# A second load queue, another split of the row means and a longer fill in the prologue of a fused attention and GLU kernel

## The chip, the cores and the metric

The kernel runs on one core of a Trainium2 chip. The metric is the time of one execution on the device in microseconds (us); a smaller number is better. The kernel before took 219.8 us in the median of three runs (219.64 to 220.88). Engines are named as the profile names them: TensorE (PE, with its weight loader PEld), VectorE (DVE), ScalarE (ACT), GpSimd (POOL) and SyncE (SP), which here issues DMA transfers.

## The reference

For 2048 tokens of width 512, in bfloat16, the reference adds three things: the input `x`, a linear attention branch and a bilinear gated branch. Both branches read the layer norm of `x`.

```python
xn = _layernorm(x)                                   # (x - mean) / sqrt(var + 1e-5)
q, k, v = split(xn @ wqkv)                           # 32 heads of 16
phi(a) = concat(softmax(a @ w_phi), softmax(-(a @ w_phi)))
kv = sum over tokens of phi(k) x v;  z = sum of phi(k)
attn = (phi(q) @ kv) / (phi(q) @ z + 1e-6) @ wo
glu  = ((xn @ w_gate) * (xn @ w_up)) @ w_down        # inner width 1792
out  = x + attn + glu
```

## The kernel before

The tokens are 16 tiles of 128 rows. All data stand in one on-chip array, `arena`, and all matrix products in eight banks of `ps`. The kernel is recorded as a list of steps, each with its engine, what it reads and writes, an estimated cost and latency; a DMA has an estimated landing time, its `at`. `_order` (L793) plays the list through with these estimates and fixes the order of the steps on every engine; a step that is marked `urgent` goes first when it could start within 300 ns (50 ns on TensorE) of the candidate. `_emit_all` (L847) then writes the instructions in that order with semaphore waits. So an estimate has no effect on the chip but through the order. In the profile nearly all matmuls have line L297, copies by ScalarE L277 and DMA issues L165 or, with a transpose, L164, as helpers record them.

The prologue is the stretch up to the first gate and up products:

- Loads (L352 to L364), all issued by SP: tile 0 of `x`, tile 1, tiles 2 and 3 together, the value weights in two halves (`wv`), the first four column blocks of the gate and up weights (`load_gu`), the feature map weights, tiles 4 to 7, and the key projection weights by a transposing DMA (`load_wT`).
- VectorE clears a block called `zero`, and TensorE multiplies it with itself 27 times into a bank that is not read (L367 to L369); four more such matmuls follow tile 1 (L734). This document calls them fills.
- For each of tiles 0 to 3 (`RAW = 4`) `emit_centred` (L418) subtracts the row mean. VectorE takes mean and variance with two instructions (L415, L416) and subtracts (L430). For tile 1 (`ACT_MEAN`) ScalarE instead takes the mean by a copy that sums its row (L423), VectorE subtracts, and the variance is taken later.
- `emit_T` (L474) transposes the centred tile by four matmuls with the identity (the prediction calls them T0 to T3), and ScalarE copies the bank to `xnT`. Later tiles are transposed by DMA.
- `k_pe` (L552) projects the tile on the value weights in four matmuls (K0 to K3 in the prediction), each of which reads a quarter of `xnT` of that tile and a quarter of `wv`; the first two need the first half of `wv`, the others the second. GpSimd raises the variance to the power of -1/2 meanwhile (L437, L439), and that scales the projection when it is copied out.
- `wprime` (L493) folds the feature map into the key projection weights.

After the prologue TensorE alternates key features, value projections and the GLU's gate and up products, later query features, and ends with the output products (`final`, L684) of all tiles.

The lines that record the fills, and those of tile 1's mean:

```python
    dve(lambda e: e.memset(zero, 0.0), [], [zero], 128)
    mms([(bank(7, 0, 128), zero, zero, True, True)] * 27, cold=True)
...
            sc.step(ACT, lambda e: e.activation(out=xn_tile(t), in_=x_tile(t), func=ACTF.Copy, scale=1.0 / 512.0,
                                                accum_out=mean),
```

Of the kernel before, what the change touches and what calls it, by code (L numbers as in the profile page):

```python
# [5 lines left out]
BF16 = mybir.dt.bfloat16  # L6
F32 = mybir.dt.float32
ACTF = mybir.ActivationFunctionType
# [4 lines left out]
PE, ACT, DVE, POOL, SP = "PE", "ACT", "DVE", "POOL", "SP"  # L13
# [6 lines left out]
NT = S_TOK // 128  # L20
NQ = D // 128
# [160 lines left out]
def bass_parallel_sum__linear_kernel_hedgehog__glu_gated_bilinear__prompt_kernel(  # L182
    nc: bass.Bass,
    A_x: bass.AP,
    A_wqkv: bass.AP,
    A_w_phi: bass.AP,
    A_wo: bass.AP,
    B_x: bass.AP,
    B_w_gate: bass.AP,
    B_w_up: bass.AP,  # L190
    B_w_down: bass.AP,
    out: bass.AP,
):
    with ExitStack() as es:
        _build(nc, es, A_x, A_wqkv, A_w_phi, A_wo, B_w_gate, B_w_up, B_w_down, out)


def _build(nc, es, A_x, A_wqkv, A_w_phi, A_wo, B_w_gate, B_w_up, B_w_down, out):
# [59 lines left out]
    def sbv(name, lo, n):  # L258
        off = layout[name] + lo
        return arena[:, off:off + n]  # L260

    def sbf(name, lo_f32, n_f32):
        off = layout[name]
        return arena[:, off:off + 2 * (lo_f32 + n_f32)].bitcast(F32)[:, lo_f32:lo_f32 + n_f32]

    def bank(b, lo=0, n=512):
        return psum[:, b * 512 + lo: b * 512 + lo + n]

    sc = _Sched(nc)


    def act_op(out_ap, in_ap, func=ACTF.Copy, scale=1.0, bias=None, prio=None):
        def fn(e):
            kw = {}
            if bias is not None:
                kw["bias"] = bias
            return e.activation(out=out_ap, in_=in_ap, func=func, scale=scale, **kw)  # L277
        r = [in_ap]
        if isinstance(scale, bass.AP):
            r.append(scale)  # L280
        if isinstance(bias, bass.AP):
            r.append(bias)
        return sc.step(ACT, fn, reads=r, writes=[out_ap], cost=(50.0 if str(in_ap.tensor.name) == "ps" else 95.0) + 0.833 * in_ap.free_size(),
                       lat=180.0, prio=prio)

    def dve(fn, reads, writes, n, rate=1.0, fixed=65.0, prio=None):
        return sc.step(DVE, fn, reads=reads, writes=writes, cost=fixed + rate * n / 0.96, lat=150.0, prio=prio)
# [4 lines left out]
    def mms(items, prio=None, cold=False):  # L292

        def fn(e):
            ins = None
            for o, l, r, a, z in items:
                ins = e.matmul(o, lhsT=l, rhs=r, start=a, stop=z)  # L297
            return ins
        reads = []
        writes = []  # L300
        c = 0.0
        for o, l, r, a, z in items:
            reads += [l, r]
            writes.append(o)
            c += max(25.0, o.free_size() / 2.4 + 2.3) * (1.92 if cold else 1.0)
        return sc.step(PE, fn, reads=reads, writes=writes, cost=c, lat=260.0, prio=prio)
# [12 lines left out]
    def x_tile(t):  # L319
        return sbv("x", t * 512, 512)  # L320

    xnT_v = sbv("xnT", 0, NQ * S_TOK).rearrange("p (q s) -> p q s", q=NQ)
# [5 lines left out]
    wv_v = sbv("wv", 0, NQ * 512).rearrange("p (q j) -> p q j", q=NQ)  # L328
# [7 lines left out]
    def load_x(on, t0, n, at):  # L336
        return sc.dma(on, sbv("x", t0 * 512, n * 512).rearrange("p (t d) -> p t d", t=n),
                      x_flat[t0 * 128:(t0 + n) * 128, :].rearrange("(t p) d -> p t d", p=128), at=at)

    def load_w(on, dst, src, at, issue=500.0):  # L340
        return sc.dma(on, dst, src, at=at, issue=issue)
# [5 lines left out]
    def load_gu(on, f0, n, at):  # L347
        return [load_w(on, v[:, :, f0 * 128:(f0 + n) * 128],
                       src[:, f0 * 128:(f0 + n) * 128].rearrange("(q p) f -> p q f", p=128), at)
                for v, src in ((wg_v, B_w_gate), (wu_v, B_w_up))]  # L350

    load_x(SP, 0, 1, 2950.0)  # L352
    load_x(SP, 1, 1, 3400.0)
    load_x(SP, 2, 2, 4700.0)
    wv_loads = [load_w(on, wv_v[:, 2 * h:2 * h + 2, :],
                       A_wqkv[h * 256:(h + 1) * 256, 1024:1536].rearrange("(q p) j -> p q j", p=128), at)
                for on, h, at in ((SP, 0, 5700.0), (SP, 1, 6600.0))]
    load_gu(SP, 0, 4, 9300.0)
    sc.dma(SP, wphi_v, bass.AP(tensor=A_w_phi.tensor, offset=A_w_phi.offset, ap=[[16, 128], [2048, NQ], [1, 16]]),
           at=10900.0)  # L360
# [3 lines left out]
    load_gu(SP, 9, 5, 22300.0)  # L364


    zero = sbv("tree", 0, 128)  # L367
    dve(lambda e: e.memset(zero, 0.0), [], [zero], 128)  # L368
    mms([(bank(7, 0, 128), zero, zero, True, True)] * 27, cold=True)  # L369


    def c_fn(e):
# [30 lines left out]
    mv_v = sbf("mv", 0, NT * 2).rearrange("p (t k) -> p t k", t=NT)  # L403
# [10 lines left out]
    def emit_moments(t):  # L414
        dve(lambda e: e.bn_stats(stats_v[:, t, 0:6], x_tile(t)), [x_tile(t)], [stats_v[:, t, 0:6]], 512)  # L415
        dve(lambda e: e.bn_aggr(mv_v[:, t, :], stats_v[:, t, 0:6]), [stats_v[:, t, 0:6]], [mv_v[:, t, :]], 6)  # L416

    def emit_centred(t):  # L418

        reads = [x_tile(t)]  # L420
        if t in ACT_MEAN:
            mean = lnt_v[:, 2, 8 + t:9 + t]
            sc.step(ACT, lambda e: e.activation(out=xn_tile(t), in_=x_tile(t), func=ACTF.Copy, scale=1.0 / 512.0,  # L423
                                                accum_out=mean),
                    reads=[x_tile(t)], writes=[xn_tile(t), mean], cost=720.0, lat=180.0)
            reads.append(xn_tile(t))
        else:
            mean = mv_v[:, t, 0:1]
            emit_moments(t)
        dve(lambda e: e.tensor_scalar(out=xn_tile(t), in0=x_tile(t), scalar1=mean, scalar2=None,  # L430
                                      op0=ALU.subtract), reads + [mean], [xn_tile(t)], 512, rate=0.5)

# [3 lines left out]
    def emit_root(t):  # L436
        pool(lambda e: e.tensor_scalar(out=veps(t), in0=mv_v[:, t, 1:2], scalar1=1e-5, scalar2=None, op0=ALU.add),  # L437
             [mv_v[:, t, :]], [veps(t)], 1)
        pool(lambda e: e.tensor_tensor(out=rstd_v[:, t, 0:1], in0=veps(t), in1=mhalf[:, 0:1], op=ALU.pow),  # L439
             [veps(t), mhalf], [rstd_v[:, t, 0:1]], 1, rate=155.0, fixed=400.0)  # L440
# [22 lines left out]
    def xn_tile(t):  # L463
        return sbv("xn", (t % 4) * 512, 512)
# [4 lines left out]
    def next_a():  # L469
        b = a_bank[0] % a_banks[0]  # L470
        a_bank[0] += 1
        return b

    def emit_T(t):  # L474
        b = (5, 6, 7, 4)[t] if t < RAW else next_a()
        mms([(bank(b, q * 128, 128), xn_tile(t)[:, q * 128:(q + 1) * 128], ident, True, True) for q in range(NQ)],
            cold=t < 2)
        act_op(xnT_v[:, :, t * 128:(t + 1) * 128], bank(b).rearrange("p (q s) -> p q s", q=NQ))

    def emit_xn(t):  # L480
        dve(lambda e: e.tensor_scalar(out=xn_tile(t), in0=x_tile(t), scalar1=mv_v[:, t, 0:1],  # L481
                                      scalar2=rstd_v[:, t, 0:1], op0=ALU.subtract, op1=ALU.mult),
            [x_tile(t), mv_v[:, t, 0:1], rstd_v[:, t, 0:1]], [xn_tile(t)], 512, rate=0.5)
        if t >= 4:
            sc.dma(SP, xnT_v[:, :, t * 128:(t + 1) * 128], xn_tile(t), transpose=True, issue=1250.0, land=3200.0,
                   at=36000.0 + 1300.0 * (t - 8) if t >= 8 else 23600.0 + 550.0 * (t - 4))
            return
        emit_T(t)
# [63 lines left out]
    def k_pe(t):  # L552
        b = next_a()
        items = group(bank(b), [(xnT(q, t * 128, 128), wv_v[:, q, :]) for q in range(NQ)])
        if t < RAW:
            for item in items:
                mms([item])
        else:
            mms(items)
        act_op(vext_all[:, t, :, 0:64], bank(b).rearrange("p (c j) -> p c j", c=8), scale=scale_of(t))  # L560
# [166 lines left out]
    for t in range(RAW):  # L727
        first = len(sc.steps)
        emit_centred(t)
        emit_T(t)  # L730
        for st in sc.steps[first:]:
            st.urgent = True
        if t == 1:
            mms([(bank(7, 0, 128), zero, zero, True, True)] * 4, cold=True).deps.append(sc.by_eng[PE][-2])  # L734
        if t in ACT_MEAN:
            emit_moments(t)
        emit_root(t)
        k_pe(t)
# [192 lines left out]
```

## Time and profile before

| what | us |
|---|---|
| median of three runs | 219.8 (219.64 to 220.88) |
| the profiled execution | 219.75 |
| its span, first instruction to last | 218.5 |
| TensorE busy, share of the span | 213.9, 98% |
| VectorE busy | 193.0, 88% |
| ScalarE busy | 115.8, 53% |
| GpSimd busy | 10.7, 5% |
| DMA moved | 19.91 MB, 91 GB/s in the mean |

The busy time of an engine is an average over stages with different limits; the profile's row of 40 slices (5.46 us each) and its chain of waits tell which engine limits a stage. A line of the chain, and one of the timeline, starts with its start and its length in us. In the timeline "x4" is the number of instructions that are merged, and what stands in brackets is the idle time of the engine before them and what ended it. The time of an overlapped group is from its first start to its last end, so a matmul's own latency is in it once.

### The profile page before, as it was taken

Reading aid. Unit: us, or ns where it says so; the run is one execution under the profiler, and the core shown is the slowest. Engines: PE = TensorE matmul, PEld = TensorE weight load, DVE = VectorE, ACT = ScalarE, POOL = GpSimd, SP = SyncE. Lnnn points to the kernel's source line nnn. Section 1 sums busy time; section 2 is a strip of 40 time slices with the busy share of each in tenths; the row PEclk is TensorE's granted clock in tenths of the full one; section 3 lists DMA queues with packets and bytes.
Section 4 is the critical chain, followed back from the end, with each engine's and each line's share of the span. In section 5 each row is a group of like instructions: output and inputs, shape, how many; then the busy total and the mean of one; then the engine's idle time right before and its main releaser. Section 6 shows DMA issues by size and latency. Waiting matters only on the chain.

```text
span 218.5 us, 3596 instructions
## 1 busy us (share of the span) xinstructions
PE 213.9 (98%) x1290; PEld 105.0 (48%) x1313; DVE 193.0 (88%) x549; ACT 115.8 (53%) x191; POOL 10.7 (5%) x29
## 2 busy tenths in 40 slices
PE   7999999999999999999999999999999999999996
PEld 7444444444445544444445544444544444454454
DVE  4577999999999389999998899999999999999532
ACT  4658987538443599965553687553444353121000
POOL 4532000010002000000000000000000000000000
DMA  6999540025900440000000002273456548546931
GB/s 172 316 238 354 100 172 4 0 52 147 329 3 13 85 99 0 0 0 3 0 0 1 3 0 48 48 99 74 96 116 128 106 110 106 123 111 126 139 76 48
DMA packets 47458, 19.91 MB, mean 91 GB/s; under 512 B 37456, under 2 KB 47440, under 8 KB 47440
## 3 DMA queue, kind: packets, MB, share of 16 engines
q1 hardware_dynamic: 47440, 19.69, 40.4%
q8 instruction: 10, 0.16, 0.3%
q14 instruction: 8, 0.07, 0.1%
HBM read 8.67 MB, written 2.10 MB: 49 GB/s over the span
## 4 chain that ended last, share of the span: by engine, by line
PE 95%; DMA 2%; issue 1%; SPq 1%; ACT 1%; DVE 0%
PE ps L297 95%; DMA arena<-in_A_wqkv_dram 2%; SPq L165 1%; ACT arena L277 1%; DVE arena L703 0%
## 5 line engine op out<-in xcount | busy, mean ns | idle before, releaser
L297 PE MATMUL ps<-arena 128*128 128x512 bf16 (+4 forms) x1290 | 213.9, 327 | 2.8 <-DVE arena L368 1.0
L297 PEld LDWEIGHTS ps<-arena 128*128 128x128 bf16 (+1 forms) x1313 | 105.0, 99 | 111.5 <-issue 1.1
L277 ACT ACTIVATE arena<-ps 128x512 bf16<-128x512 f32 (+1 forms) x136 | 71.8, 583 | 47.1 <-PE ps L297 40.2
L277 ACT ACTIVATE arena<-arena 128x1024 bf16<-128x1024 bf16 (+1 forms) x40 | 38.5, 977 | 30.1 <-DVE arena L528 29.9
L542 DVE TENSOR_TENSOR arena<-arena 128x512 f32<-128x512 bf16 (+3 forms) x128 | 48.8, 392 | 0.2
L598 DVE TENSOR_TENSOR arena<-ps,arena 128x512 bf16<-128x512 f32 x56 | 38.3, 683 | 5.8 <-PE ps L297 4.7
L522 DVE TENSOR_TENSOR arena<-arena 128x64 bf16<-128x64 bf16 (+3 forms) x128 | 31.5, 271 | 3.8 <-ACT arena L277 3.5
L528 DVE TENSOR_TENSOR arena<-arena 128x1024 bf16<-128x1024 bf16 x32 | 21.7, 680 | 0.1
L703 DVE TENSOR_TENSOR arena<-ps,arena 128x512 bf16<-128x512 f32 (+2 forms) x13 | 8.3, 642 | 7.1 <-PE ps L297 7.1
L574 DVE TENSOR_TENSOR arena<-arena 128x1024 bf16<-128x1024 bf16 x16 | 10.8, 678 | 0.0
L277 ACT ACTIVATE arena<-ps,arena 128x512 bf16<-128x512 f32 x12 | 7.8, 681 | 2.6 <-PE ps L297 2.6
L571 DVE RECIPROCAL arena<-arena 128x64 bf16<-128x64 f32 x16 | 8.7, 544 | 0.0
L675 DVE TENSOR_TENSOR arena<-ps,arena 128x512 bf16<-128x512 f32 x12 | 8.1, 678 | 0.1
L452 DVE BATCH_NORM_STATS2 arena<-arena 128x6 f32<-128x512 bf16 x12 | 8.0, 684 | 0.0
L667 DVE RECIPROCAL arena<-ps 128x32 f32<-128x32 f32 x16 | 5.6, 349 | 1.8 <-PE ps L297 1.8
L654 DVE TENSOR_TENSOR arena<-arena 128x512 bf16<-128x512 bf16 x16 | 6.6, 415 | 0.0
L651 DVE RECIPROCAL arena<-arena 128x32 f32<-128x32 f32 x16 | 5.4, 338 | 0.0
L481 DVE TENSOR_SCALAR arena<-arena 128x512 bf16<-128x512 bf16 x12 | 4.3, 400 | 0.7 <-POOL arena L460 0.7
L415 DVE BATCH_NORM_STATS2 arena<-arena 128x6 f32<-128x512 bf16 x4 | 2.8, 690 | 2.1 <-DMA arena<-in_A_x_dram 2.0
L458 POOL TENSOR_SCALAR arena<-arena 128x4 f32<-128x4 f32 x3 | 0.8, 257 | 52.2 <-DVE arena L454 52.2
L460 POOL TENSOR_TENSOR arena<-arena 128x4 f32<-128x4 f32 x3 | 3.1, 1049 | 0.2
L700 DVE SCALAR_TENSOR_TENSOR arena<-ps,arena 128x512 bf16<-128x512 f32 x4 | 3.0, 748 | 0.1
(29 smaller groups left out, 24.4 us busy)
## 6 DMA issues: line engine op xcount, KB each, us to landing
out_dram<-arena SPq DMA_DIRECT2D x15, 128.0 KB, 1.9
arena<-in_B_w_down_dram SPq DMA_DIRECT2D x1, 1792.0 KB, 7.5
arena<-in_B_w_gate_dram SPq DMA_DIRECT2D x2, 640.0 KB, 6.6
arena<-in_B_w_up_dram SPq DMA_DIRECT2D x2, 640.0 KB, 7.8
arena<-in_A_x_dram SPq DMA_DIRECT2D x1, 1024.0 KB, 5.7
arena<-arena SPq DMA_TRANSPOSE x44, 2.6
arena<-in_A_wqkv_dram SPq DMA_DIRECT2D x2, 256.0 KB, 3.9
arena<-in_B_w_gate_dram SPq DMA_DIRECT2D x1, 512.0 KB, 5.7
```

The costliest lines, as they stand in the source:

```text
L277: return e.activation(out=out_ap, in_=in_ap, func=func, scale=scale, **kw)
L297: ins = e.matmul(o, lhsT=l, rhs=r, start=a, stop=z)
L452: dve(lambda e, t=t: e.bn_stats(stats_v[:, t, 0:6], x_tile(t)), [x_tile(t)], [stats_v[:, t, 0:6]], 512)
L522: dve(lambda e, dst=dst, src=src, k=k: e.tensor_tensor(out=dst, in0=src[:, :, 0:k], in1=src[:, :, k:2 * k], op=ALU.max), [src], [dst], 16 ...
L528: dve(lambda e: e.tensor_tensor(out=p4, in0=p4, in1=src[:, :, None, :].to_broadcast([128, 16, 16, 4]), op=ALU.subtract), [pst, src], [pst] ...
L542: dve(lambda e, dst=dst, src=src, k=k: e.tensor_tensor(out=dst, in0=src[:, :, 0:k], in1=src[:, :, k:2 * k], op=ALU.add), [src[:, :, 0:2 * ...
L571: dve(lambda e: e.reciprocal(out=rs, in_=sm), [sm], [rs], 64, rate=6.0)
L574: dve(lambda e: e.tensor_tensor(out=e4, in0=e4, in1=r4[:, :, None, :].to_broadcast([128, 16, 16, 4]), op=ALU.mult), [ek_v[:, t, :], rs], [ ...
L598: dve(lambda e: e.tensor_tensor(out=dst, in0=bank(bu), in1=gr, op=ALU.mult), [bank(bu), gr], [dst], 512, prio=-1.0)
L654: dve(lambda e: e.tensor_tensor(out=e1, in0=e1, in1=rs[:, :, None, :].to_broadcast([128, 8, 16, 4]), op=ALU.mult), [e1, rs], [e1], 512, ra ...
L675: dve(lambda e: e.tensor_tensor(out=o4, in0=n4, in1=w4, op=ALU.mult), [nd[:, :, 0:64], w], [o], 512)
L703: dve(lambda e: e.tensor_tensor(out=og, in0=ob, in1=xs, op=ALU.add), [ob, xs], [og], c1 - c0, prio=-2.0)
```

## The change

- Tile 2 and tile 3 of `x` are loaded apart. Tile 3 and the second half of the value weights are issued by ScalarE, behind a one-element copy that the change puts first on ScalarE (`first`); both DMAs wait for this copy. The estimated landing times of these loads change with it.
- The fills read a constant of ones that is there from the program's start, and VectorE's clear goes. There are 32 instead of 27 at the start, and two behind T0 and two behind T1 instead of four behind T1.
- For tile 1 ScalarE takes the negative mean and subtracts it in a second activation; VectorE's subtraction of that tile goes.
- The copy of a transposed tile to `xnT` is made in two halves of 256 columns each.

```diff
--- before.py
+++ after.py
@@ -349,12 +349,18 @@
                        src[:, f0 * 128:(f0 + n) * 128].rearrange("(q p) f -> p q f", p=128), at)
                 for v, src in ((wg_v, B_w_gate), (wu_v, B_w_up))]
 
+    def load_v(on, h, at):
+        return load_w(on, wv_v[:, 2 * h:2 * h + 2, :],
+                      A_wqkv[h * 256:(h + 1) * 256, 1024:1536].rearrange("(q p) j -> p q j", p=128), at)
+
     load_x(SP, 0, 1, 2950.0)
     load_x(SP, 1, 1, 3400.0)
-    load_x(SP, 2, 2, 4700.0)
-    wv_loads = [load_w(on, wv_v[:, 2 * h:2 * h + 2, :],
-                       A_wqkv[h * 256:(h + 1) * 256, 1024:1536].rearrange("(q p) j -> p q j", p=128), at)
-                for on, h, at in ((SP, 0, 5700.0), (SP, 1, 6600.0))]
+    load_x(SP, 2, 1, 4000.0)
+    first = sc.step(ACT, lambda e: e.activation(out=sbf("lnt", 2 * NT + 15, 1), in_=nc.const_aps.tensor(1.0, [128, 1], BF16),
+                                                func=ACTF.Copy), writes=[sbf("lnt", 2 * NT + 15, 1)], cost=1350.0)
+    load_x(ACT, 3, 1, 4400.0).deps.append(first)
+    load_v(SP, 0, 5300.0)
+    load_v(ACT, 1, 5800.0).deps.append(first)
     load_gu(SP, 0, 4, 9300.0)
     sc.dma(SP, wphi_v, bass.AP(tensor=A_w_phi.tensor, offset=A_w_phi.offset, ap=[[16, 128], [2048, NQ], [1, 16]]),
            at=10900.0)
@@ -364,9 +370,8 @@
     load_gu(SP, 9, 5, 22300.0)
 
 
-    zero = sbv("tree", 0, 128)
-    dve(lambda e: e.memset(zero, 0.0), [], [zero], 128)
-    mms([(bank(7, 0, 128), zero, zero, True, True)] * 27, cold=True)
+    one = nc.const_aps.tensor(1.0, [128, 128], BF16)
+    mms([(bank(7, 0, 128), one, one, True, True)] * 32, cold=True)
 
 
     def c_fn(e):
@@ -420,13 +425,14 @@
         reads = [x_tile(t)]
         if t in ACT_MEAN:
             mean = lnt_v[:, 2, 8 + t:9 + t]
-            sc.step(ACT, lambda e: e.activation(out=xn_tile(t), in_=x_tile(t), func=ACTF.Copy, scale=1.0 / 512.0,
+            sc.step(ACT, lambda e: e.activation(out=xn_tile(t), in_=x_tile(t), func=ACTF.Copy, scale=-1.0 / 512.0,
                                                 accum_out=mean),
                     reads=[x_tile(t)], writes=[xn_tile(t), mean], cost=720.0, lat=180.0)
-            reads.append(xn_tile(t))
-        else:
-            mean = mv_v[:, t, 0:1]
-            emit_moments(t)
+            sc.step(ACT, lambda e: e.activation(out=xn_tile(t), in_=x_tile(t), func=ACTF.Identity, bias=mean),
+                    reads=[x_tile(t), xn_tile(t), mean], writes=[xn_tile(t)], cost=522.0, lat=180.0)
+            return
+        mean = mv_v[:, t, 0:1]
+        emit_moments(t)
         dve(lambda e: e.tensor_scalar(out=xn_tile(t), in0=x_tile(t), scalar1=mean, scalar2=None,
                                       op0=ALU.subtract), reads + [mean], [xn_tile(t)], 512, rate=0.5)
 
@@ -475,7 +481,8 @@
         b = (5, 6, 7, 4)[t] if t < RAW else next_a()
         mms([(bank(b, q * 128, 128), xn_tile(t)[:, q * 128:(q + 1) * 128], ident, True, True) for q in range(NQ)],
             cold=t < 2)
-        act_op(xnT_v[:, :, t * 128:(t + 1) * 128], bank(b).rearrange("p (q s) -> p q s", q=NQ))
+        for q in range(0, NQ, 2):
+            act_op(xnT_v[:, q:q + 2, t * 128:(t + 1) * 128], bank(b, q * 128, 256).rearrange("p (q s) -> p q s", q=2))
 
     def emit_xn(t):
         dve(lambda e: e.tensor_scalar(out=xn_tile(t), in0=x_tile(t), scalar1=mv_v[:, t, 0:1],
@@ -730,8 +737,8 @@
         emit_T(t)
         for st in sc.steps[first:]:
             st.urgent = True
-        if t == 1:
-            mms([(bank(7, 0, 128), zero, zero, True, True)] * 4, cold=True).deps.append(sc.by_eng[PE][-2])
+        if t < 2:
+            mms([(bank(7, 0, 128), one, one, True, True)] * 2, cold=True).deps.append(sc.by_eng[PE][-2])
         if t in ACT_MEAN:
             emit_moments(t)
         emit_root(t)
```

## The prediction

> **What bounds the kernel now.** I read the chain that ended last first, then the page's busy row of TensorE, then the timeline of the first 16 us, engine by engine, because the diff touches nothing that runs later.
>
> The chain over the whole span, as the page shares it out, and the page's busy row:
>
> ```profile
> PE   7999999999999999999999999999999999999996
> ...
> PE 95%; DMA 2%; issue 1%; SPq 1%; ACT 1%; DVE 0%
> ```
>
> TensorE is full in every slice but the first and the last, and 95% of the chain is its matmuls. Nothing in the diff changes how many matmuls run after the prologue, so the change is worth what it takes from, or adds to, the time at which TensorE starts its unbroken run. The chain cut to the first 25 us shows where that lies:
>
> ```profile
> 2.69 4.46 DMA arena<-in_A_wqkv_dram
> ...
> 7.20 0.82 PE ps L297 x3
> ...
> 8.08 6.66 PE ps L297 x33
> 14.76 0.61 ACT arena L277
> ...
> 15.45 9.66 PE ps L297 x44
> ```
>
> The last wait of the prologue is the second half of the value weights (wv1): issued at 2.69, landed 4.46 later. From 7.20 TensorE runs without a real hole; the stop at 14.76 is the copy of the folded weights, which the change leaves as it is. The timeline gives the feeders:
>
> ```profile
> 0.78 1.28 ACT L423 ACT_TABLE_LOAD   x1 [0.78 <-PEq L916]
> 1.03 3.06 PE L297 MATMUL ps<-arena 128*128 128x128 bf16 x27 [1.03 <-DVE arena L368]
> 2.18 0.98 SPq L165 DMA_DIRECT2D arena<-in_A_wqkv_dram  x2
> 3.39 0.63 ACT L423 ACTIVATE arena<-arena 128x512 bf16<-128x512 bf16 x1 [1.33 <-DMA arena<-in_A_x_dram]
> 3.89 0.68 DVE L430 TENSOR_SCALAR arena<-arena 128x512 bf16<-128x512 bf16 x2
> 3.92 0.19 ACT L423 ACTIVATION_READ_ACCUMULATOR arena<-arena 128x1 f32 x1
> 4.69 0.69 DVE L415 BATCH_NORM_STATS2 arena<-arena 128x6 f32<-128x512 bf16 x1
> 5.64 0.35 DVE L430 TENSOR_SCALAR arena<-arena 128x512 bf16<-128x512 bf16 x1
> 7.20 7.03 PEld L297 LDWEIGHTS ps<-arena 128*128 128x128 bf16 x37 [0.45 <-DMA arena<-in_A_wqkv_dram]
> 10.03 4.20 PEld L297 LDWEIGHTS ps<-arena 128*128 128x128 bf16 x20
> 14.65 0.90 PEld L297 LDWEIGHTS ps<-arena 64*128 64x128 bf16 x35 [0.42 <-issue]
> ```
>
> And three narrow cuts of TensorE give its two speeds:
>
> ```profile
> 5.34 0.42 PE L297 MATMUL ps<-arena 128*128 128x128 bf16 x2
> 5.70 0.94 PE L297 MATMUL ps<-arena 128*128 128x512 bf16 x2
> 8.08 0.39 PE L297 MATMUL ps<-arena 128*128 128x128 bf16 x4
> ```
>
> Two early 128-column matmuls span 0.42, and the 27 fills give (3.06-0.31)/26 = 0.106 apart; four late ones in 0.39 are 0.056 apart. The 512-column pair at 5.70 is 0.38 apart, three at 7.20 in 0.82 are 0.216 apart. So the array doubles its pace at about 6.45; the granted clock reads 1.00 throughout and does not show it. The weight loader's 0.45 before 7.20 is its wait for wv1. In order: T0, T1 (transposes of x 0 and x 1) from 4.30 to 5.13, four fills, value projection K0 from 5.70, T2, a hole from 6.92 to 7.20, T3 at 8.08, then nine K matmuls, 8.30+9x0.216 = 10.24, where the first gate matmul starts (its weights load from 10.03). The 20 gate and up matmuls then reach 14.56. Every microsecond by which 10.24 moves, the end moves, as long as the up weights (issued at 3.72, 6.9 to landing: 10.6) and the transposed key weights are there.
>
> **The change, part by part.** Order first, from the planner's own rules worked by hand (for order alone): fills, T0, two fills, T1, two fills, T2, K0 (4), one of K1, T3, the rest of K1, K2, K3, gate. T2 goes ahead of K0 because it is marked urgent and due within the planner's 0.05. The gate's planned start hardly moves, so the order behind it should stay.
>
> *Fills on ones.* The clear on VectorE (0.87 to 0.98) goes; TensorE need not wait until 1.03 but can start at about 0.80, since the other engines' first instructions start at 0.78. 32 fills at 0.107 end at 4.22, before T0 can start at 4.30; started at 1.03 they would end at 4.45 and cost 0.15. I take nothing, nearest to the 0.78 rows. The hole 3.89 to 4.30 closes. Whether a closed hole doubles the pace earlier no row shows: between nothing and all cold work after 4.30. I take nothing, the pace doubling at 6.45 again.
>
> The Trainium skill, in "TensorE: Matmul & The Clock Gate" (Part 1), says that the clock gate opens after a busy window of about 3.4 us, that the window runs free and that the point moves by 0.5 us from run to run. By it the closed hole is no promise: this trace doubled about 5.4 after its first matmul, hole and all.
>
> *x 2 apart.* x 2 and x 3 came in one 256 KB load, issued at 1.71 and 3.0 to landing (4.7), and stats of x 2 waited for it until 4.69. 128 KB alone, by x 1's spacing (0.44 behind x 0), lands at about 3.8. VectorE also loses x 1's subtraction, so stats 2 starts when x 0's is through, 4.22: stats 0.69, aggregate 0.18, subtract 0.35 with gaps as now give 5.52 instead of 5.99, and x 3 6.79 instead of 7.20. x 3 comes from ScalarE's issue at about 2.4 plus 2.1 to 3.0 (the x rows), 4.5 to 5.4: beside stats 2 until about 5.49, and it costs if later.
>
> *Second half of wv and x 3 on ScalarE.* Table load to 2.06, the small copy 0.23 (the 128x65 copy's row), x 3's issue 0.42, wv1's 0.47, with gaps: ScalarE is free at about 3.3, x 1 lands at 3.37, so the mean starts at 3.39 as now. Behind these two issues on ScalarE stand x 1's mean and subtraction, for which T1 and everything behind it wait: that is the cover, 0.07 thick. SP passes one issue less, so gate and up weights, key-projection weights, x 4 to 7 and the long transpose issue 0.5 earlier; bytes bind there (290 GB/s from 3.5 to 6.5, 333 to 10.5), so I give them nothing. wv1's issue moves from 2.69 to about 2.85, but it no longer queues behind wv0: x 2, x 3 and both halves are 768 KB, at 290 to 333 GB/s from 3.4 all in by 5.8 to 6.1. K0's third matmul is due at 6.64, so the hole at 6.92 goes. If wv1 is as late as now (7.16), 0.5 of it returns.
>
> *Mean 1 and subtraction on ScalarE.* The accumulator is read by 4.11; a second 512-wide activation is 0.63 (SBUF row) and 0.09 for its per-partition operand (0.688 against 0.597 on L277): 4.15 to 4.87. The subtraction leaves VectorE (0.35). T1 may start at 4.92 instead of 4.70; the first two fills fill 4.71 to 4.92.
>
> *Copies in halves.* A copy of 512 columns is 0.60, its successor 0.49 later; a half is between 0.30 and 0.40. The first half of x 0's copy is ready at about 5.35 instead of 5.55, but K0 now waits for T2, so no gain; the extra 0.07 per tile on ScalarE lies beside TensorE.
>
> *Sum.* T1 4.93 to 5.35, fills to 5.57, T2 (ready 5.57) slow to 6.00, K0's first at 6.00, second at 6.42, third (fast) at 6.64, fourth 6.86, K1's first 7.07, T3 7.29 to 7.51, eleven K matmuls 2.37: 9.88. Against 10.24 that is 0.36 earlier. The up weights are needed at 10.75 and landed at 10.6; the folding at 14.30 needs the transposed weights, on hand before 14.65 and issued 0.5 earlier. Span 218.5 becomes 218.15; the profiled execution took 219.75, 1.25 more than its span and 0.05 under the median, so I forecast 219.4.
>
> **Rivals.** *ScalarE is late (slower, 0.18).* The trace shows ScalarE idle from 2.06 to 3.39; it shows no instruction that could have started in between. If the engine accepts nothing until up to 3.39, then copy and two issues run to 4.55, the mean to 5.30, the subtraction to 6.06, T1 at 6.11 with TensorE empty from 4.92. From there 0.43 (T1), 0.11, 0.22, K and T3 3.67: 10.54, 0.30 late, and wv1, issued at 4.1 and 3.4 to 4.5 to landing (the two wv rows), comes 7.5 to 8.6 where 7.30 is wanted. Together 0.3 to 1.3 late, near 220.4. It decides from the point at which ScalarE is free 0.36 later than 3.39. Against it: x 1 landed at 3.37, which explains the wait by itself.
>
> The Trainium skill, "ScalarE: Activation LUTs" (What ACT_TABLE_LOAD costs), speaks for this one: it puts a drain of about 1.38 us behind the load's 1.283. The load agrees to the digit; the drain would end at 3.44, where the trace starts an ACTIVATE at 3.39, so at most 1.33 fits, and no row can show less.
>
> *Issue slower on ScalarE, or wv1 late: no gain (0.19).* The issues on L165 took 0.40 to 0.89; at 0.6 to 0.65 each ScalarE is free at 3.7 and the 0.36 is gone. wv1 at 7.16 leaves 0.1 to 0.2 at best. 219.6 to 219.9.
>
> *The pace doubles early (0.12).* If the closed hole brings it by 5, T2 ends at 5.8, all K at 0.216: 9.45. The gate runs to 10.31, the up weights hold it to 10.3 to 10.6: 0.5 to 0.8 gained, 218.9 to 219.2.
>
> *Not what it says, or another order behind (0.03).*
>
> **Chances.** Forecast 219.1 to 219.6: 0.48. A measurement tells about 1% from no change, 2.2 us: 217.6 and 222.0. The prologue holds no 2.2 to win (its holes and slow matmuls after 4.30 are under 1.5), and the slow rival ends at 221.0; so 0.02 faster, 0.93 within, 0.05 slower for what I have not seen. Range 218.9 to 220.7: from the early pace to most of the late ScalarE.
>
> **What would show it.** Right: first gate weights load near 9.7 instead of 10.03, no hole before K0's third matmul, mean 1 on ScalarE at 3.4, stats 2 at 4.2. Wrong: ScalarE's first DMA issue later than 2.6, T1 after 5.0, wv1 landing after 6.6, or a hole anywhere behind 15 us.

## The result

The changed kernel took 222.48 us in the median of eight runs (220.99 to 225.26), the kernel before 219.88 (219.47 to 220.88): 1.0096 times as long, with a 95% interval of 1.0074 to 1.0118. (One run, 225.26, is left out of the ratio as disturbed.) The forecast was 219.4, with a range that ended at 220.7. The profiled execution took 222.71 with a span of 221.5, which is 3.0 more than the span before.

The page's row of TensorE and its clock row, of the kernel after:

```profile
PE   8699999999999999999999999999999999999996
...
PEclk9799999999999999999999999999999999999999
```

The holes are still in the first two slices alone, but there is a clock row now: the page before had none. The chain cut to the first 22 us (start, length, what):

```profile
0.78 1.28 ACT L359
...
2.08 0.21 ACT arena L359
...
2.31 0.39 ACTq L165
...
2.73 5.58 DMA arena<-in_A_wqkv_dram
8.31 0.14 issue
8.45 13.56 PE ps L297 x87
```

It runs through the moved load from end to end: table load, small copy, issue of x 3, and then the second half of the value weights (wv1), issued at 2.73, as before (2.69), and landed 5.58 later instead of 4.46. The timeline has the rest:

```profile
3.67 0.63 ACT L428 ACTIVATE arena<-arena 128x512 bf16<-128x512 bf16 x1 [1.39 <-DMA arena<-in_A_x_dram]
4.22 0.69 DVE L420 BATCH_NORM_STATS2 arena<-arena 128x6 f32<-128x512 bf16 x1
5.21 0.40 PE L297 MATMUL ps<-arena 128*128 128x128 bf16 x4 [0.20 <-ACT arena L431]
6.16 0.69 DVE L420 BATCH_NORM_STATS2 arena<-arena 128x6 f32<-128x512 bf16 x1 [0.65 <-DMA arena<-in_A_x_dram]
6.45 0.59 PE L297 MATMUL ps<-arena 128*128 128x512 bf16 x2 [0.48 <-DMA arena<-in_A_wqkv_dram]
8.45 13.78 PE L297 MATMUL ps<-arena 128*128 128x512 bf16 x88 [1.41 <-DMA arena<-in_A_wqkv_dram]
17.59 4.36 PEld L297 LDWEIGHTS ps<-arena 64*128 64x128 bf16 x51 [0.42 <-issue]
```

TensorE made the first two matmuls of K0 at 6.45 and then had nothing until 8.45. The folding of the key weights starts at 17.59 instead of 14.65: 2.94 late, which is the whole loss of the span. Stretches of the same kernel (from:to length, busy time of PE, PEld, DVE, ACT, POOL, then the granted clock, DMA share and GB/s):

```profile
6.90:8.45 1.55, 0.14 (x1) 0.03 (x1) 1.51 (x6) 0.00 (x0) 0.95 (x2) 0.89 1.08 369
8.45:11.40 2.95, 2.95 (x11) 1.28 (x12) 0.20 (x2) 1.35 (x3) 1.26 (x4) 0.50 1.28 302
11.40:17.50 6.10, 6.10 (x29) 2.69 (x27) 2.39 (x4) 3.25 (x5) 1.13 (x3) 0.99 0.97 277
```

The wait is followed by 3 us at a granted clock of 0.50. So the loss of this execution has two parts: TensorE waited until 8.45, and then it ran at half pace. The second part is not in every execution: over the whole span the clock averaged 0.992 in three runs (222.71 to 223.29) and 1.000 in the four from 220.99 to 222.25. The transfer engines were not idle meanwhile: 369 GB/s, but more than half of it for other data. Their packets from 6.0 to 7.5 by queue (q1 is SyncE's, q10 ScalarE's):

```profile
q1 hardware_dynamic: 306, 0.31, 61.4%
q10 hardware_dynamic: 222, 0.22, 43.6%
```

The first half of the value weights had landed at 6.3, so what q1 moved from then on are the loads issued behind it, the gate weights first.

### The profile page after: what moved, and what is told of

The parts are those of the page before. It is cut to its first block, busy times and chain, and to the rows that moved or that the text cites. A ratio compares the mean times of both kernels' runs of the same rounds, so it can differ in the third digit from the quotient of the medians.

```text
span 221.5 us, 3634 instructions
## 1 busy us (share of the span) xinstructions
PE 216.7 (98%) x1318; PEld 105.6 (48%) x1318; DVE 192.5 (87%) x547; ACT 117.1 (53%) x197; POOL 10.7 (5%) x29
## 4 chain that ended last, share of the span: by engine, by line
PE 95%; DMA 3%; ACT 1%; ACTq 0%; DVE 0%; issue 0%
PE ps L297 95%; DMA arena<-in_A_wqkv_dram 3%; ACT L359 1%; ACTq L165 0%; DVE arena L710 0%; ACT arena L359 0%
## 5 line engine op out<-in xcount | busy, mean ns | idle before, releaser
L297 PE MATMUL ps<-arena 128*128 128x512 bf16 (+5 forms) x1282 | 213.0, 329 | 2.1 <-DMA arena<-in_A_wqkv_dram 1.9
L297 PEld LDWEIGHTS ps<-arena 128*128 128x128 bf16 (+1 forms) x1282 | 102.0, 98 | 113.0 <-issue 4.3
L277 ACT ACTIVATE arena<-ps 128x512 bf16<-128x512 f32 (+2 forms) x140 | 71.9, 570 | 45.9 <-PE ps L297 37.9
L297 PE MATMUL ps<-const-bfloat16-1.0 128*128 128x128 bf16 x36 | 4.1, 300 | 0.8 <-PEq L923 0.8
L297 PEld LDWEIGHTS ps<-const-bfloat16-1.0 128*128 128x128 bf16 x36 | 3.7, 140 | 0.8 <-issue 0.8
```

## The experiments

Times of the kernel before beside them are 219.74 to 219.89. wv1 names the second half of the value weights; past the prologue the order of the steps is that of the changed kernel or of the kernel before, as the edit starts from the one or the other (`gate_waits` excepted).

**The change without its loads** (`rest_only`, from the changed kernel)

```diff
-    first = sc.step(ACT, ...)
-    load_x(ACT, 3, 1, 4400.0).deps.append(first)
+    load_x(SP, 3, 1, 4400.0)
     load_v(SP, 0, 5300.0)
-    load_v(ACT, 1, 5800.0).deps.append(first)
+    load_v(SP, 1, 5800.0)
```

> The changed kernel with all its loads issued by SyncE again, in the order x 0, x 1, x 2, x 3, value weights first half, second half; the one-element copy on ScalarE goes, all else of the change stays. Theory (the queue): the loss is all in the second half of the value weights, which on ScalarE's queue landed at 8.3 instead of 7.2. Here it lands between 6.3 and 7.2, the third matmul of the first projection starts by 7.3, and the time is 219.3 to 219.9, up to 0.4 under the kernel before. Rival (the rest costs: mean on ScalarE, copies in halves, fills): it stays above 220.5 with the loads back.

220.10 (219.57 to 221.03, 12 runs), ratio 1.0004 (0.9988 to 1.0020). The loss is gone with the loads, so fills, mean and halved copies did not cause it. But the gain that I had expected with them is missing too, and the time lies just above the expected 219.3 to 219.9: wv1 landed at 7.16, no earlier than before, and TensorE waited 0.80 for it.

**The loads without the rest** (`loads_only`, from the kernel before)

```diff
-    load_x(SP, 2, 2, 4700.0)
-    wv_loads = [... for on, h, at in ((SP, 0, 5700.0), (SP, 1, 6600.0))]
+    load_x(SP, 2, 1, 4000.0)
+    first = sc.step(ACT, ...)
+    load_x(ACT, 3, 1, 4400.0).deps.append(first)
+    load_v(SP, 0, 5300.0)
+    load_v(ACT, 1, 5800.0).deps.append(first)
```

> The kernel before with the loads of the change alone (x 2 and x 3 apart, x 3 and the second half of the value weights on ScalarE behind the one-element copy). Theory (the queue): the second half lands at about 8.3, TensorE is empty from about 6.9 to 8.4, and the time is 221.0 to 222.7. Rival (the rest costs): within 0.4 of the kernel before.

223.17 (220.59 to 223.80, 4 runs), ratio 1.0116 (1.0068 to 1.0163). The loads alone make the loss. Chain and two stretches of this kernel:

```profile
2.74 6.43 DMA arena<-in_A_wqkv_dram
9.17 0.05 issue
9.22 12.99 PE ps L297 x84
```

```profile
7.50:9.20 1.70, 0.00 (x0) 0.00 (x0) 1.24 (x6) 0.60 (x1) 1.17 (x4) 0.94 1.10 349
9.20:12.50 3.30, 3.28 (x11) 1.46 (x12) 0.00 (x0) 1.19 (x2) 1.20 (x4) 0.51 1.18 211
```

wv1 lands at 9.17, even later than I expected, and the clock is 0.51 for 3.3 us behind the wait. The time, too, is above the expected 221.0 to 222.7.

**wv1 back on SyncE, x 3 left on ScalarE** (`wv1_on_sp`, from the changed kernel)

```diff
-    load_v(ACT, 1, 5800.0).deps.append(first)
+    load_v(SP, 1, 5800.0)
```

> The changed kernel with the second half of the value weights issued by SyncE, behind the first half; x 3 stays on ScalarE. Theory (the queue hurts what TensorE waits for first): the second half lands at 6.3 to 7.3, x 3 still at about 6, which VectorE feels as 0.6 of waiting and TensorE as at most 0.2; 219.3 to 220.2. Rival (any load on a second queue slows the start of all): the second half lands after 7.5 and the time is above 220.7.

219.57 (219.50 to 220.05, 10 runs), ratio 0.9981 (0.9967 to 0.9995): one line moves the kernel by 2.9 us, from worse than before to a little better than both kernels.

```profile
2.17 3.89 DMA arena<-in_A_wqkv_dram
6.07 0.14 issue
6.20 18.89 PE ps L297 x118
```

The chain now goes through the first half (landed 6.07); wv1, issued at 2.7, came 4.0 later, at 6.6, and from 6.20 TensorE runs on. The folding starts at 14.42, 0.23 before the 14.65 of the kernel before.

**TensorE kept busy in the wait** (`fills_in_wait`, from the changed kernel)

```diff
             for i, item in enumerate(items):
                 mms([item])
+                if (t, i) == (0, 1):
+                    mms([(bank(5, 0, 128), one, one, True, True)] * 28).cost = 0.0
```

> The changed kernel with 28 more fills (1.6 us at the fast pace) behind the second matmul of the first projection, in the hole in which TensorE waits for the second half of the value weights. The loads stay as changed. Theory (clock): the hole let the array fall back to the slow pace until 11.4; kept busy, it runs at 0.216 for each 512-column matmul from the landing at 8.4 on, and the time is 220.8 to 221.3 with little scatter. Rival (no part for the pace): 222.0 to 222.8 as the changed kernel, or more for the added fills.

221.31 (220.81 to 221.39, 7 runs), ratio 1.0047 (1.0029 to 1.0064). The 28 added fills do no useful work and make the kernel 1.2 faster. Timeline of TensorE, and a stretch:

```profile
6.97 1.81 PE L297 MATMUL ps<-const-bfloat16-1.0 128*128 128x128 bf16 x28
8.62 0.59 PE L297 MATMUL ps<-arena 128*128 128x512 bf16 x2
```

```profile
8.60:11.50 2.90, 2.90 (x21) 1.47 (x19) 0.18 (x1) 2.12 (x5) 1.55 (x4) 1.00 1.24 273
```

The loads are as late as in the changed kernel (wv1 lets TensorE go on at 8.62), but the clock stays at 1.00 behind the wait, and it averaged 1.000 in all seven runs, against four of eight of the changed kernel. So the half pace is a second loss, which comes with the emptiness of TensorE in the wait and not with the late landing as such. It does not follow every such wait; the next experiment has one without it.

**The gate weights on ScalarE's queue, wv1 on SyncE** (`gate_on_act`, from the changed kernel)

```diff
+    def load_one(on, v, src, f0, n, at):
...
-    load_v(ACT, 1, 5800.0).deps.append(first)
-    load_gu(SP, 0, 4, 9300.0)
+    load_v(SP, 1, 5800.0)
+    load_one(ACT, wg_v, B_w_gate, 0, 4, 9300.0).deps.append(first)
+    load_one(SP, wu_v, B_w_up, 0, 4, 9300.0)
```

> The changed kernel with the second half of the value weights back on SyncE, behind the first half, and the gate weights (512 KB) on ScalarE's queue behind x 3 in its place; the up weights stay on SyncE. Theory (two queues share the transfer engines about evenly, so what is issued later on the other queue takes half): the second half, though on SyncE, lands late again, 7.3 to 8.0, against 6.6 with x 3 alone on ScalarE's queue, and the gate weights land by 8.9 or earlier; 220.0 to 222. Rival (ScalarE's queue itself is slow and hurts only what is on it): the second half lands at 6.4 to 6.8 as with x 3 alone there, the gate weights late, after 9.5.

220.19 (219.53 to 221.03, 10 runs), ratio 0.9999 (0.9977 to 1.0021). The profiled execution is the slowest of the ten (221.03). In it wv1 landed at 8.1, 5.5 after its issue: later than the theory wanted, and far from the rival's 6.4 to 6.8, although it did not go through ScalarE's queue. The gate weights landed at 9.2, later than the theory and earlier than the rival wanted. Packets from 6.0 to 7.0 by queue, and TensorE:

```profile
q10 hardware_dynamic: 317, 0.32, 97.1%
q1 hardware_dynamic: 41, 0.03, 9.3%
```

```profile
8.28 6.00 PE L297 MATMUL ps<-arena 128*128 128x512 bf16 x30 [1.53 <-DMA arena<-in_A_wqkv_dram]
```

```profile
6.70:8.30 1.60, 0.07 (x2) 0.05 (x2) 1.53 (x7) 0.00 (x0) 0.95 (x2) 1.00 1.08 367
8.30:10.40 2.10, 2.10 (x13) 1.07 (x14) 0.35 (x3) 1.49 (x4) 0.79 (x2) 1.00 1.13 310
```

The first half (6.0) and x 3 (6.1) had landed, so in this microsecond q10 moved the gate weights, issued 0.08 after wv1, and q1 hardly anything of wv1. Here it is the bytes on the other queue that make wv1 late, whichever queue wv1 is on; but the two queues do not share evenly, as the theory had it. Four of the ten runs took 219.5 to 219.7, as `wv1_on_sp` does, so wv1 is probably not so late in those; no trace of one was taken. The wait of 1.53 is no shorter than the 1.41 of the changed kernel, and the clock stayed at 1.00 behind it.

**SyncE's gate and up weights wait for wv1** (`gate_waits`, from the changed kernel)

```diff
-    load_v(ACT, 1, 5800.0).deps.append(first)
-    load_gu(SP, 0, 4, 9300.0)
+    second = load_v(ACT, 1, 5800.0)
+    second.deps.append(first)
+    for load in load_gu(SP, 0, 4, 9300.0):
+        load.deps.append(second)
```

> The changed kernel, but SyncE issues the gate and up weights only when the second half of the value weights has landed; it is still on ScalarE's queue. All of SyncE's later loads move back with them, so the time (some us more) says nothing; what is read is the landing. Theory (sharing): with nothing beside it from about 6.3 on, and less before, the second half lands at 5.9 to 6.8 instead of 8.3. Rival (the queue itself is slow): 7.8 or later.

223.91 (one run). wv1 landed at 7.8, the rival's number; but the planner had moved the feature map weights, x 4 to 7 (512 KB) and the key weights ahead of the waiting loads, so another competitor had taken the place of the gate weights. Inconclusive, and repeated without that fault:

**Everything that SyncE issues behind the first half waits for wv1** (`hold_all`, from the changed kernel)

```diff
+    second = load_v(ACT, 1, 5800.0)
+    second.deps.append(first)
...
+    for load in held:
+        load.deps.append(second)
```

`held` are the gate and up weights, the feature map weights, x 4 to 7, the key weights and the later gate and up weights.

> The changed kernel, but every load that SyncE issues behind the first half of the value weights waits until the second half, still on ScalarE's queue, has landed; the order on every engine is that of the changed kernel. The later loads come some 4 us later, so the time, 223 to 226, says nothing; what is read is the landing of the second half. Theory (it was the gate weights, issued by SyncE 0.08 before it, that took its share): with nothing of SyncE's behind the first half in flight it lands at 6.2 to 7.0 instead of 8.3. Rival (the second queue itself is slow): 7.8 or later.

220.87 (one run). Chain and TensorE's timeline:

```profile
2.31 0.39 ACTq L165
2.70 0.04 issue
2.73 3.80 DMA arena<-in_A_wqkv_dram
```

```profile
5.89 0.59 PE L297 MATMUL ps<-arena 128*128 128x512 bf16 x2
6.67 3.43 PE L297 MATMUL ps<-arena 128*128 128x512 bf16 x18 [0.19 <-DMA arena<-in_A_wqkv_dram]
10.49 0.82 PE L297 MATMUL ps<-arena 128*128 128x512 bf16 x3 [0.39 <-DMA arena<-in_B_w_gate_dram]
```

The same load, on the same queue, issued at the same 2.73, lands at 6.53 instead of 8.31 when nothing that SyncE issues behind the first half is in flight beside it. The other traces with the loads of the change have 8.33 (`fills_in_wait`) and 9.17 (`loads_only`). So 1.8 of its 5.58 came from these later loads, the gate weights first, which SyncE issued 0.08 earlier. The 18 matmuls from 6.67 (the remaining 14 of K0 to K3, and T3) end in a last one that started at 10.10-0.38 = 9.72, so the gate could have started at 9.93. The kernel as a whole is slow here because the gate and up weights now come late (TensorE went on at 10.49 and at 12.20); it is still faster than the 223 to 226 that I expected.

**All loads on SyncE, x 3 behind the first half** (`x3_behind_wv0`, from the changed kernel)

```diff
-    first = sc.step(ACT, ...)
-    load_x(ACT, 3, 1, 4400.0).deps.append(first)
     load_v(SP, 0, 5300.0)
-    load_v(ACT, 1, 5800.0).deps.append(first)
+    load_x(SP, 3, 1, 4400.0)
+    load_v(SP, 1, 5800.0)
```

> The changed kernel with all loads on SyncE in the order x 0, x 1, x 2, value weights first half, x 3, second half; no one-element copy. Theory (only the order of bytes ahead of what TensorE wants next counts): first half at about 5.2, x 3 at about 5.6, second half 6.3 to 7.2; 219.3 to 220.1, as with all loads in the old order (220.1) or up to 0.5 better, and not clearly better than with x 3 alone on ScalarE (219.6), since there SyncE has one issue less ahead of the gate weights.

220.61 (220.23 to 221.00, 12 runs), ratio 1.0023 (1.0008 to 1.0039): slower than expected. The first half did come early, at 5.0, but wv1 only at 7.4.

**x 3 on ScalarE, nothing else of the change** (`x3_act_only`, from the kernel before)

```diff
-    load_x(SP, 2, 2, 4700.0)
-    wv_loads = [... for on, h, at in ((SP, 0, 5700.0), (SP, 1, 6600.0))]
+    load_x(SP, 2, 1, 4000.0)
+    first = sc.step(ACT, ...)
+    load_x(ACT, 3, 1, 4400.0).deps.append(first)
+    load_v(SP, 0, 5300.0)
+    load_v(SP, 1, 5800.0)
```

> The kernel before, with x 2 and x 3 loaded apart and x 3 alone on ScalarE behind the one-element copy; both halves of the value weights on SyncE, and the fills, the mean and the copies as before. It asks where the 0.3 of the kernel with the second half on SyncE (219.57) came from. If from the loads: 219.4 to 219.8 here, with the second half landed by 6.8. If from the fills, the mean or the halves: 219.8 to 220.2, as the kernel before.

219.80 (219.44 to 221.55, 12 runs), ratio 1.0017 (0.9989 to 1.0044). The interval hides that there are two groups: eight runs from 219.44 to 219.93 and four from 221.38 to 221.55. In the profiled execution (219.49) wv1 landed at 6.5, as expected from the loads. The first group is as good as `wv1_on_sp`, so its gain comes with the loads; the second group is not seen there in ten runs.

**The same with the change's longer fill** (`x3_act_fills`)

```diff
-    dve(lambda e: e.memset(zero, 0.0), [], [zero], 128)
-    mms([(bank(7, 0, 128), zero, zero, True, True)] * 27, cold=True)
+    mms([(bank(7, 0, 128), one, one, True, True)] * 32, cold=True)
...
-            mms([(bank(7, 0, 128), zero, zero, True, True)] * 4, ...
+            mms([(bank(7, 0, 128), one, one, True, True)] * 4, ...
```

> The kernel before with x 3 alone on ScalarE, as in the run before this one, and the fills of the change at the start (32 on ones, from 0.8 on; four behind T1 as before). A third of the runs with the old fills took 221.4 to 221.6 instead of 219.4 to 219.9. If those are runs in which the array reached its full pace one window of 3.4 us late, because the fills began at 1.03 and paused from 3.9 to 4.3, then with the longer fills they are gone or rare: 219.4 to 220.1 in all. If they come from the transfers, they stay, a third of the runs or so.

219.65 (219.37 to 220.24, 12 runs), ratio 0.9993 (0.9979 to 1.0007). No run of the second group is left, none of twelve against four of twelve. So the longer, unbroken fill may have a use: to take away runs that cost 1.8 more. The two sets were run at different times and on different chips, so the fill is not shown to be the cause. That those are runs with a late full pace fits the size and this outcome, but no trace of one was taken, so that is not shown either.

## Why the prediction was wrong

**The landing of wv1, the step that failed.** I let x 2, x 3 and both halves share the engines, "768 KB at 290 to 333 GB/s from 3.4 all in by 5.8 to 6.1", and took it as a gain that wv1 "no longer queues behind wv0". The sum left out the gate weights, 512 KB, and the up weights behind them: on one queue they are issued behind wv1; on two queues they run beside it. wv1 landed at 8.31, and at 6.53 with SyncE's later loads held back. (Even then it was 0.4 behind my 6.1: the transfers were through by 6.0, and the landing showed half a microsecond later, which my sum did not have.) The change did not bring wv1 forward, it gave up its place in front of the gate weights. I had priced the rest of that step ("if wv1 is as late as now, 0.5 of it returns") only down to the landing of before; a later wv1 stood only in the rival of a late ScalarE, and there by a late issue (4.1), not by a longer way from issue to landing. This step alone carries the time out of the range: the four runs with a mean clock of 1.000 took 220.99 to 222.25, and the range ended at 220.7.

The Trainium skill, "DMA: Bandwidth & Descriptors" (Queues, rings and completion order), states that each transfer engine goes round between the queues it has work for. The 0.31 MB and 0.22 MB of q1 and q10 in the same 1.5 us agree in that both were served at once; the 0.32 and 0.03 MB of `gate_on_act` show that the shares need not be even. Against this step of the prediction I did not hold that rule.

**The pace, the term that I took as nothing.** I wrote that the pace would double at 6.45 "again" and asked only whether earlier. In the profiled execution it doubled much earlier, at 4.65 (the fourth matmul of T0 starts the fast spacing), and then fell back: the clock of 0.89 over 6.90 to 8.45 means about 0.34 at one half, from 8.1 on, and it is 0.50 until about 11.5. That I did not ask what TensorE's own waiting does to its clock is the second fault. The two together make the sum of this execution: the third matmul of K0 at 8.45 instead of the forecast 6.64 is 1.81; from there to the gate took 13.18-8.45 = 4.73 (17.59 less the 20 matmuls and the gap, 4.41, as before) instead of 9.88-6.64 = 3.24, which is 1.49. Together 3.30, and 9.88+3.30 = 13.18, where the gate started. With the wait alone the gate would start at 8.45+3.24 = 11.69, 1.45 later than the 10.24 of before; `fills_in_wait`, which has the wait and not the half pace, took 1.44 more than the kernel before beside it (221.31 against 219.87).

When the pace doubles is not settled by the kernel. With the same fills, and T0 started at the same 4.38, T0 ran at the full pace in the trace of `gate_on_act` and at half in that of `fills_in_wait`:

```profile
4.38 0.40 PE L297 MATMUL ps<-arena 128*128 128x128 bf16 x4 [0.30 <-DVE arena L441]
4.38 0.61 PE L297 MATMUL ps<-arena 128*128 128x128 bf16 x4
```

So 4.65 belongs to that one execution, and my rival of an early pace asked for something that closing the hole does not ensure.

The Trainium skill's "TensorE: Matmul & The Clock Gate" (Part 1), which I weighed only for the fill, gives windows of 3.4 us. Doubling at 4.65, the drop near 8.1 and the next doubling near 11.5 are 3.4 apart, and the trace agrees. The page speaks of an idle window; here TensorE was busy for 1.67 of the 3.42 us from 4.69 to 8.11, and the clock dropped all the same. That the windows run free would also explain why only some runs have the drop: 0.992 in the mean is one window at half pace (3.4x0.5/222 = 0.008). It does not explain the whole spread: one run of `loads_only` took 223.80 at a mean clock of 1.000.

**ScalarE late, my slower rival.** It fell with the first lines of the trace: the small copy started at 2.08, 0.02 behind the table load, x 3's issue took 0.39 and wv1's 0.46, and ScalarE was free at 3.2. It then waited for x 1, which landed 0.28 later than before (mean at 3.67 instead of 3.39); that is of this execution, for in `fills_in_wait`, with the same loads, the mean started at 3.35. The drain of 1.38 us behind a table load, for which I cited the Trainium skill's "ScalarE: Activation LUTs" (What ACT_TABLE_LOAD costs), is not there behind this first load: 0.02 decides. That this rival had the right sign, slower, is luck: its mechanism was wrong.

**What held.** x 2 alone let its stats start at 4.22, as forecast. T1 started at 5.21 instead of 4.93, by x 1's late landing, and T2 at 5.57, as forecast. x 3 came later than my 4.5 to 5.4, at 6.1 (stats at 6.16). With wv1 in time the sum was near: the gate could start at 9.93 in `hold_all`, against 9.88, and `wv1_on_sp` folds at 14.42, against 14.30, and took 219.57, against 219.4. The order behind the prologue stayed, and no hole came up behind 15 us.

**Fills, mean and halves.** Together, with the loads in the old queue, they moved the median by nothing that can be told (1.0004). If the closed hole earns its place, it is by the runs that it may spare, not by the typical one.

## What to carry to other kernels

A load on a second queue isn't ahead of anything: the order in which loads are issued ranks them only within one queue, and beside it the other queue takes its share for whatever it holds, needed soon or not. So put on the second queue what can be late (in `wv1_on_sp` x 3 came at 5.9, and TensorE waited only 0.33, for the first half), keep what the bottleneck waits for first at the head of the first queue, and count all bytes in flight beside it, those needed last too. Where TensorE must wait for microseconds near its start, price the wait twice: once as a wait, and once as the half pace that can follow; with harmless matmuls in the wait none of seven runs had the second part.

## What was not expected of the hardware

With all six early loads on one queue, x 2 and x 3 apart, the transfers themselves slackened while wv1 was due. Stretches of 1 us of `rest_only`, `x3_behind_wv0` and `wv1_on_sp`; the last number is GB/s:

```profile
5.50:6.50 1.00, 1.00 (x8) 0.37 (x6) 0.93 (x4) 1.00 (x5) 0.76 (x3) 1.00 0.73 152
```

```profile
5.00:6.00 1.00, 1.00 (x13) 1.00 (x12) 0.68 (x3) 1.00 (x4) 0.78 (x2) 1.00 0.70 155
```

```profile
5.50:6.50 1.00, 0.67 (x9) 0.33 (x6) 0.61 (x1) 1.00 (x5) 0.58 (x2) 1.00 0.98 336
```

The first two moved 152 and 155 GB/s while loads were queued; the kernel before moved 261 from 5.5 to 6.5. The stretch stands just ahead of wv1 (7.16 and 7.37), and what was not moved in it, 336-152 GB/s for 1 us, is 0.18 MB or about 0.5 us at 336 (an estimate), the distance to the 6.6 of `wv1_on_sp`. The kernels with x 3 on ScalarE have a slack of their own, but earlier: from 3.50 to 4.25 they moved 107 to 146 GB/s, `rest_only` 250 and the kernel before 359. In the three traces with x 3 alone on the second queue the first half came later for it (5.9 to 6.3, against 5.0 to 5.7 with one queue) and wv1 earlier (6.5 to 6.9, against 7.2 to 7.4). Why the transfers slacken was not tried and stays open. Also, 128 KB of x took 2.1 to 2.6 from issue to landing as one of the first three loads on the first queue, and 3.5 to 3.9 on the second, in every kernel that loads x 3 there, the one with everything else held back among them.
